# Attention of batch 0 in a fused attention and MLP kernel: split casts of x, the last exp and its sums in halves, reordered evictions and W1 copies, first MLP matmuls in two rows

## The chip, the cores and the metric

The kernel runs on one core of one Trainium2 chip. The metric is device time in microseconds (us), the median of several executions. TensorE is called PE here, VectorE DVE, ScalarE ACT, GpSimd POOL. PE multiplies matrices into PSUM banks; DVE and ACT move results out of PSUM ("evictions"); POOL does elementwise work and issues most of the loads.

A ratio is the mean time of one kernel's fast runs over the mean of the other's fast runs of the same rounds, so it is not quite the ratio of the medians that stand beside it.

## The reference, cut to what matters

```python
# attention, for each batch and head: 512 tokens x against 32 state rows, D = 64
scores = (x @ state.T) / sqrt(D);  a = softmax(scores);    xread = a @ state
scores2 = (state @ x.T) / sqrt(D); a2 = softmax(scores2);  sread = a2 @ x
h_in = concat(xread, sread)            # 544 rows per batch, 8 heads * 64 = 512 columns
# MLP
h = h_in @ w_in                        # 512 -> 2048
out = (h * sigmoid(h)) @ w_out         # 2048 -> 512
```

There are 8 batches. The kernel never forms xread: it folds state and w_in into a matrix W1 per batch, and multiplies W1 by the transposed attention weights aT. So the first MLP matmuls of a batch need both aT (two halves of four heads each, `hg` 0 and 1) and W1.

## The kernel before

Batch 0 has nothing to hide behind. Its attention is laid out at the start, as a chain over all engines:

```python
    keep_busy(7, psH, "h1")             # 7 filler matmuls of 128x512 on PE
    ...                                 # cast of the state, 4 PE transposes, 4 DVE copies to stT
    keep_busy(4, psH, "h1")
    cast_x(0, nc.vector, h0=0, nh=4)    # first half of x (4 heads), float32 to bf16, 1024 columns
    pe_transpose_x(0, 0, 2, <psO>)      # 8 PE transposes into 2 banks; copies: DVE one, ACT one
    cast_x(0, nc.vector, h0=4, nh=4)    # second half
    ...
    scores(0, 0)
    exps(0, 0)                          # ACT, 512 columns
    pe_transpose_x(0, 1, 2, <psH>)      # again one copy on DVE, one on ACT
    scores(0, 1)
    exps(0, 1)
    nc.scalar.activation(warm[:], warm[:], func=SILU, bias=0.0)   # loads the SILU table
    norm(0, 0)                          # DVE sum and reciprocal, POOL multiply of 512 columns
    norm(0, 1, ((nc.gpsimd, 0, 2), (nc.vector, 2, 2)))            # multiply: half POOL, half DVE
    w1_cols(0, [(0, 256)], (nc.scalar, nc.scalar))
    ...                                 # four weight loads and the load of x(1), issued by POOL
    keep_busy(4, psO, "o")
    pe_transpose_a(0, 0, nc.vector)     # 4 PE transposes, one DVE copy to aT
    pe_transpose_a(0, 1, nc.vector)
```

The MLP of batch 0 follows:

```python
    for ft in range(NFT):               # 16 tiles of 128 hidden columns
        upto(min(ft + LEAD0[ft], ready))       # h tile = two matmuls (hg 0, hg 1), then SILU on ACT
        if ft in W0:
            w1_cols(0, [W0[ft]], both)         # next block of W1; one copy on DVE, one on ACT
        if ft == 1:
            token_sums(0)                      # two DVE reductions of 1 us, then two small ones
        if ft == 4:
            sread(0)                           # 18 matmuls, then a DVE reciprocal and 4 products
        if ft == 5:
            transpose_state()
        if ft == 6:
            evict_state(0, nc.vector)
        if ft == 8:
            evict_state(1, nc.vector)
        ...
            for tt in range(3):
                G2(0, tt, ft)                  # second MLP matmul
```

Each engine is read here as running its own instructions in the order of the program; experiment 4 shows it for DVE, where a sum whose input was ready at 7.86 us started only at 9.05, behind two copies.

The softmax here doesn't subtract the row's maximum and nothing guards it: scores larger than these inputs give would overflow.

## Time and profile before

| | before |
|---|---|
| median of 6 runs | 224.67 us (224.41 to 225.01) |
| span of the profiled run | 222.8 us |
| PE busy | 213.7 us, 96% |

PE is busy nearly all the time, and part of the busy time at the start is filler matmuls, so the attention of batch 0 is a place where its time is not useful work. The first part of the page of the kernel before, busy time of each engine with share of the span:

```profile
PE 213.7 (96%) x1491; PEld 101.2 (45%) x1491; DVE 104.7 (47%) x183; ACT 142.5 (64%) x241; POOL 46.1 (21%) x64
```

The chain of work that ended last, in order of time, kernel before. Columns: start and length in us, then engine, what it wrote, its line in the kernel, and how many instructions are merged:

```profile
1.22 3.17 PE ps_busy L129 x7
...
4.61 1.82 PE ps_busy L129 x4
...
8.04 0.60 ACT exp_nat L242
...
9.57 0.61 ACT exp_nat L242
...
10.20 0.70 DVE rs L252
...
11.32 0.80 POOL an L255
...
12.16 0.41 PE ps_at L272 x4
...
12.60 0.43 DVE aT L123
...
13.07 0.81 PE h L362 x3
13.88 0.31 PE ps_w L336 x8
...
14.61 1.90 DVE es_f L282 x2
...
17.28 0.61 DVE W L123
...
17.94 0.39 PE h L362
```

Read it from the bottom. The MLP tile at 17.94 (the fifth, "tile 4") waited for a W1 copy on DVE. That copy stood in the DVE queue behind the token sums (`es_f`). The queue had started with the W1 block at 13.88, and that block stands on PE behind all four matmuls of the first two h tiles, which waited for the second half of aT. So tile 4 hangs on the end of batch 0's attention through PE's order and the DVE queue.

What PE waited for from 12 to 30 us, kernel before (total us, times, longest):

```profile
PE ps_at L272 <- POOL an L255: 0.8, 1, 0.8
PE ps_w L336 <- DVE stT L123: 0.4, 1, 0.4
PE h L362 <- DVE W L123: 0.4, 1, 0.4
PE h L362 <- DVE aT L123: 0.3, 1, 0.3
...
```

### The profile page before, as it was taken

What the parts mean: (1) busy time and instruction counts of PE and PEld (TensorE: products, weight loads), DVE (VectorE), ACT (ScalarE), POOL (GpSimd) and SP (SyncE); (2) the same over time, 40 slices, a digit from 0 to 9 for tenths busy, and PEclk for the clock granted to TensorE, in tenths of its full rate; (3) what the DMA queues carried; (4) which work ended last, traced back from release to release, by engine and by line L of the source; (5) the groups of instructions that cost most, each with busy time, mean ns of one, the idle gap of its engine ahead of it and who ended that gap; (6) DMA issues with size and microseconds to landing.
All of it is one profiled execution on the core that took longest, in us unless ns stands there. A gap on an engine that the chain in (4) does not pass through costs nothing.

```text
span 222.8 us, 3748 instructions
## 1 busy us (share of the span) xinstructions
PE 213.7 (96%) x1491; PEld 101.2 (45%) x1491; DVE 104.7 (47%) x183; ACT 142.5 (64%) x241; POOL 46.1 (21%) x64
## 2 busy tenths in 40 slices
PE   7879899999989999999999999999999999999993
PEld 2425235445425443544444444444454445466652
DVE  4665846452975165525644382629260846010011
ACT  2555469899555985589567947695759675834410
POOL 8480001800810035001800090008000300000000
PEclk9999999999999999999999999999999999999998
DMA  6999955493376116911495138503700330111112
GB/s 184 198 205 206 211 190 174 159 228 113 96 233 139 47 47 121 306 47 47 100 250 125 50 94 242 136 3 105 177 18 35 85 108 0 47 47 50 47 47 94
DMA packets 32209, 26.78 MB, mean 120 GB/s; under 512 B 20160, under 2 KB 26048, under 8 KB 32192
## 3 DMA queue, kind: packets, MB, share of 16 engines
q1 hardware_dynamic: 25376, 14.75, 23.8%
q0 software_dynamic: 6816, 11.80, 23.6%
q8 instruction: 11, 0.18, 0.3%
q14 instruction: 6, 0.05, 0.1%
HBM read 17.37 MB, written 8.91 MB: 118 GB/s over the span
## 4 chain that ended last, share of the span: by engine, by line
PE 85%; DVE 10%; ACT 1%; issue 1%; POOL 0%; DVEq 0%; POOLq 0%
PE o L391 45%; PE h L362 24%; PE ps_w L336 4%; PE h L372 3%; PE ps_busy L129 2%; DVE es_f L282 2%; PE ps_sc L230 2%; PE o_half L413 2%; DVE rb L312 2%; PE ps_sr L303 1%; DVE stT L123 1%; DVE W L123 1%; DVE xmT L316 1%; DVE rs L252 1%; ACT exp_nat L242 1%
## 5 line engine op out<-in xcount | busy, mean ns | idle before, releaser
L391 PE MATMUL o<-w_out_sb,g 128*128 128x512 bf16 x512 | 137.6, 379 | 0.0
L383 ACT ACTIVATE g<-h 128x512 bf16<-128x512 f32 (+1 forms) x144 | 82.1, 574 | 41.4 <-PE h L362 27.2
L362 PE MATMUL h<-aT,W 128*128 128x512 bf16 x256 | 75.5, 379 | 1.9 <-DVE W L123 1.5
L391 PEld LDWEIGHTS <-g 128*128 128x128 bf16 x528 | 49.7, 98 | 58.2 <-issue 6.4
L123 DVE COPY o_sb<-o 128x512 f32<-128x512 f32 x17 | 11.8, 692 | 62.7 <-PE o L391 62.5
L362 PEld LDWEIGHTS <-W 128*128 128x128 bf16 x256 | 24.6, 98 | 32.3 <-DVE W L123 3.7
L255 POOL TENSOR_TENSOR an<-exp_nat,rc 128x512 bf16<-128x512 bf16 (+1 forms) x16 | 16.0, 1010 | 109.8 <-DVE rc L253 109.6
L123 DVE CAST W<-ps_w 128x512 bf16<-128x512 f32 (+1 forms) x31 | 20.0, 675 | 18.7 <-PE ps_w L336 18.7
L121 ACT ACTIVATE W<-ps_w 128x512 bf16<-128x512 f32 (+1 forms) x35 | 18.7, 575 | 11.4 <-PE ps_w L336 11.3
L312 DVE RECIPROCAL rb<-ps_sr 128x256 f32<-128x256 f32 x8 | 14.0, 1749 | 16.2 <-PE ps_sr L303 16.2
L121 ACT ACTIVATE o_sb<-o 128x512 f32<-128x512 f32 x15 | 8.9, 596 | 14.3 <-PE o L391 6.1
L282 DVE TENSOR_REDUCE es_f<-exp_nat 128x128 f32<-128x512 bf16 x16 | 15.5, 1011 | 0.2
L100 POOL CAST x_nat<-x_f 128x512 bf16<-128x512 f32 x24 | 14.7, 648 | 0.0
L336 PE MATMUL ps_w<-w_in_sb,stT 64*32 64x512 bf16 (+1 forms) x264 | 11.7, 376 | 0.6 <-DVE stT L123 0.4
L252 DVE TENSOR_REDUCE rs<-exp_nat 128x16 f32<-128x512 bf16 x16 | 10.6, 660 | 1.9 <-ACT exp_nat L242 1.2
L95 POOL DMA_DIRECT2D x_f<-in_x_dram x7 | 6.5, 926 | 19.8 <-DVE x_nat L100 18.3
L316 DVE TENSOR_TENSOR xmT<-ps_sr,rb 64x64 bf16<-64x64 f32 x32 | 9.6, 299 | 0.6
L372 PE MATMUL h<-xmT,w_in_sb 128*128 128x256 bf16 x64 | 9.6, 272 | 0.0
L242 ACT ACTIVATE exp_nat<-ps_sc 128x512 bf16<-128x512 f32 x16 | 8.8, 594 | 0.9 <-PE ps_sc L230 0.8
L372 PEld LDWEIGHTS <-w_in_sb 128*128 128x128 bf16 x64 | 6.3, 98 | 3.9
L242 ACT ACT_TABLE_LOAD x6 | 7.7, 1283 | 0.1
L537 ACT ACT_TABLE_LOAD x6 | 7.7, 1283 | 0.1
(56 smaller groups left out, 102.7 us busy)
## 6 DMA issues: line engine op xcount, KB each, us to landing
out_dram<-o_sb SPq DMA_DIRECT2D x33, 256.0 KB, 2.4
x_f<-in_x_dram POOLq DMA_DIRECT2D x7, 1024.0 KB, 6.7
w_in_sb<-in_moe_w_in_dram POOLq DMA_DIRECT2D x3, 512.0 KB, 10.2
w_out_sb<-in_moe_w_out_dram POOLq DMA_DIRECT2D x3, 512.0 KB, 12.0
x_f<-in_x_dram SPq DMA_DIRECT2D x2, 512.0 KB, 4.5
w_in_sb<-in_moe_w_in_dram POOLq DMA_DIRECT2D x2, 256.0 KB, 7.3
w_out_sb<-in_moe_w_out_dram POOLq DMA_DIRECT2D x2, 256.0 KB, 7.8
st_b<-in_state_dram POOLq DMA_DIRECT2D x1, 256.0 KB, 12.1
```

The lines of the kernel that those rows point to most:

```text
L100: eng.tensor_copy(x_nat[b][:, ds(c0, nc_), ds(h0, nh), :], x_f[:, ds(h0, nh), ds(c0, nc_), :].rearrange("p h c d -> p c h d"),)
L121: nc.scalar.activation(dst, src, func=COPY, bias=0.0)
L123: eng.tensor_copy(dst, src)
L242: nc.scalar.activation(e[:], sc_ps[hg][:], func=EXP, bias=0.0, scale=SCALE)
L255: eng.tensor_tensor(a[:, ds(c, n)], e[:, ds(c, n)], rc[:, ds(c, n)].to_broadcast([128, n, 4, NS]), op=MULT,)
L282: nc.vector.tensor_reduce(f[:, hg], exp_nat[b, hg].rearrange("p c s n -> p s n c"), axis=AX, op=ADD)
L312: nc.vector.reciprocal(rb[:], ps[:, 1, :, :, :])
L336: nc.tensor.matmul(pss[f, hg][ds(32 * s, 32), 0:n], stT[ds(r, 64), b, h // 2, s % 2, :], w_in_sb[ds(r, 64), h // 2, ds(f, n)], start=True, ...
L362: nc.tensor.matmul(ps[:], W1[b][:, hg, ds(128 * ft, 128)], aT[b][:, hg, :, :], start=(hg == 0), stop=(hg == 1), skip_group_check=True,)
L372: nc.tensor.matmul(ps[:, 0:256], w_in_sb[:, kt, ds(128 * ft, 128)], xmT[:, :, kt].rearrange("p t n b -> p t (n b)"), start=(kt == 0), stop ...
L383: nc.scalar.activation(g[:, 0:n], ps[:, 0:n], func=SILU, bias=0.0)
L391: nc.tensor.matmul(outs[tt][:], gt[b * NFT + ft][:, ds(128 * tt, 128)], w_out_sb[:, ft, :], start=(ft == 0), stop=(ft == NFT - 1), skip_gr ...
```

## The change

The intent is to shorten the attention of batch 0. Both casts of batch 0's x are split in two, so that transposes can start on the first part; the exps and sums of the last half are cut in halves, so that the sum overlaps the exp. The evictions of the second half's transposes all go to DVE, W1's first copies go ahead of the SILU table load, POOL gets less of the last multiply. The fillers are moved rather than saved: 7 and 4 at the front become 4 and 5, and 2 are put in ahead of the last transposes (15 in both kernels). The first row (hg 0) of the first two h tiles is put ahead of the wait for the second half of aT.

```diff
-        eng.tensor_copy(
+        copy(
+            eng,                       # in cast_x: ACT can now do it too
@@
-    keep_busy(7, psH, "h1")
+    keep_busy(4, psH, "h1")
@@
-    keep_busy(4, psH, "h1")
+    keep_busy(5, psH, "h1")
@@
-    cast_x(0, nc.vector, h0=0, nh=4)
+    cast_x(0, nc.vector, 0, 2, 0, 4)
+    cast_x(0, nc.scalar, 2, 2, 0, 4)
     pe_transpose_x(0, 0, 2, ...)
-    cast_x(0, nc.vector, h0=4, nh=4)
+    cast_x(0, nc.vector, 0, 2, 4, 4)
+    cast_x(0, nc.vector, 2, 2, 4, 4)
@@
+    def g1_half(k, hg):                # one row (hg) of h tile k
+        b, ft = divmod(k, NFT)
+        if hg == 0:
+            h_ps[k] = psH.tile([128, 512], FP32, tag="h1", name="h1")
+        nc.tensor.matmul(h_ps[k][:], W1[b][:, hg, ...], aT[b][:, hg, :, :],
+                         start=(hg == 0), stop=(hg == 1), ...)
@@
+    pe_transpose_x(0, 1, 2, new_h, (nc.vector, nc.vector), (0,))
     scores(0, 0)
     exps(0, 0)
-    pe_transpose_x(0, 1, 2, ...)
+    pe_transpose_x(0, 1, 2, new_h, (nc.vector, nc.vector), (1,))
     scores(0, 1)
-    exps(0, 1)
+    exps(0, 1, 2)                      # in two halves
+    norm(0, 0)
+    norm(0, 1, ((nc.vector, 0, 3), (nc.gpsimd, 3, 1)), 2)    # sums in two halves
+    w1_cols(0, [(0, 256)], (nc.scalar, nc.scalar))
     nc.scalar.activation(warm[:], warm[:], func=SILU, bias=0.0)
-    norm(0, 0)
-    norm(0, 1, ((nc.gpsimd, 0, 2), (nc.vector, 2, 2)))
-    w1_cols(0, [(0, 256)], (nc.scalar, nc.scalar))
@@
     keep_busy(4, psO, "o")
     pe_transpose_a(0, 0, nc.vector)
+    keep_busy(2, psO, "o")
     pe_transpose_a(0, 1, nc.vector)
+    g1_half(0, 0)
+    g1_half(1, 0)
```

More of the change, by code (lines that the diff above doesn't have):

```diff
@@ L172, with pe_transpose_x @@
             )
-    keep_busy(4, psH, "h1")
-    def pe_transpose_x(b, hg, nb=2, new=bank, engs=(nc.vector, nc.scalar)):
+    keep_busy(5, psH, "h1")
+    def pe_transpose_x(b, hg, nb=2, new=bank, engs=(nc.vector, nc.scalar), only=None):
         if b not in xT:
@@ L181, in pe_transpose_x @@
         m = 4 // nb
-        for u in range(nb):
+        for u in range(nb) if only is None else only:
             ps = new([128, m, 2, 128], BF16, "ps_xt")
@@ L237, in scores, with exps, norm @@
                 )
-    def exps(b, hg):
+    def exps(b, hg, n=4):
         e = att.tile([128, 4, 4, NS], BF16, tag="exp", name="exp_nat")
         exp_nat[b, hg] = e
-        nc.scalar.activation(e[:], sc_ps[hg][:], func=EXP, bias=0.0, scale=SCALE)
+        for c in range(0, 4, n):
+            nc.scalar.activation(
+                e[:, ds(c, n)], sc_ps[hg][:, ds(c, n)], func=EXP, bias=0.0, scale=SCALE
+            )
     an = {}
-    def norm(b, hg, parts=((nc.gpsimd, 0, 4),)):
+    def norm(b, hg, parts=((nc.gpsimd, 0, 4),), nr=4):
         e = exp_nat[b, hg]
@@ L251, in norm @@
         an[b, hg] = a
-        nc.vector.tensor_reduce(rs[:], e[:], axis=AX, op=ADD)
+        for c in range(0, 4, nr):
+            nc.vector.tensor_reduce(rs[:, ds(c, nr)], e[:, ds(c, nr)], axis=AX, op=ADD)
         nc.vector.reciprocal(rc[:], rs[:])
@@ L355 @@
     outs = {}
+    h_ps = {}
+    def g1_half(k, hg):
+        b, ft = divmod(k, NFT)
+        if hg == 0:
+            h_ps[k] = psH.tile([128, 512], FP32, tag="h1", name="h1")
+        nc.tensor.matmul(
+            h_ps[k][:],
+            W1[b][:, hg, ds(128 * ft, 128)],
+            aT[b][:, hg, :, :],
+            start=(hg == 0),
+            stop=(hg == 1),
+            skip_group_check=True,
+        )
     def emit_G1(k):
         b, ft = divmod(k, NFT)
-        ps = psH.tile([128, 512], FP32, tag="h1", name="h1")
         if b < B:
-            for hg in range(2):
-                nc.tensor.matmul(
-                    ps[:],
-                    W1[b][:, hg, ds(128 * ft, 128)],
-                    aT[b][:, hg, :, :],
-                    start=(hg == 0),
-                    stop=(hg == 1),
-                    skip_group_check=True,
-                )
+            if k not in h_ps:
+                g1_half(k, 0)
+            g1_half(k, 1)
+            ps = h_ps.pop(k)
         else:
+            ps = psH.tile([128, 512], FP32, tag="h1", name="h1")
             for kt in range(4):
@@ L432, in upto @@
             done[0] += 1
+    new_h = lambda sh, dt, nm: psH.tile(sh, dt, tag="h1", name=nm)
+    pe_transpose_x(0, 1, 2, new_h, (nc.vector, nc.vector), (0,))
     scores(0, 0)
     exps(0, 0)
-    pe_transpose_x(0, 1, 2, lambda sh, dt, nm: psH.tile(sh, dt, tag="h1", name=nm))
+    pe_transpose_x(0, 1, 2, new_h, (nc.vector, nc.vector), (1,))
     scores(0, 1)
-    exps(0, 1)
+    exps(0, 1, 2)
+    norm(0, 0)
+    norm(0, 1, ((nc.vector, 0, 3), (nc.gpsimd, 3, 1)), 2)
+    w1_cols(0, [(0, 256)], (nc.scalar, nc.scalar))
     nc.scalar.activation(warm[:], warm[:], func=SILU, bias=0.0)
-    norm(0, 0)
-    norm(0, 1, ((nc.gpsimd, 0, 2), (nc.vector, 2, 2)))
-    w1_cols(0, [(0, 256)], (nc.scalar, nc.scalar))
     load_w_in(1024)
```

## The prediction

> **What bounds the kernel now.** The page gives TensorE (PE) 213.7 of 222.8 us busy; only idle or filler PE time can be won. The change touches batch 0 before 15 us. There the chain that ended last (in order of time) runs: fillers `ps_busy` x7 to 4.39, state transposes to 4.60, fillers x4 to 6.42, x transposes, an ACT copy of xT 7.06-7.66, scores, exp 8.04-8.64, ACT copy of xT 8.63-9.19, scores, exp 9.57-10.17, DVE sum 10.20-10.90, reciprocal to 11.19, POOL multiply 11.32-12.12, transposes, DVE copy of aT 12.60-13.03, first MLP matmuls 13.07.
>
> **What the change removes and moves (timeline durations).**
> 1. Fillers 7 to 4, then 4 to 5. State transposes can start at about 3.1 instead of 4.32, since the state cast ends at 2.98. The x transposes start near 5.4 instead of 6.22. The first half of x lands at about 4.8; its cast, halved over DVE and ACT, takes about 0.42 and 0.60 instead of 0.69.
> 2. But PE now transposes the second half's first two chunks before scores(0,0). That half of x lands only at about 7.16 (the DVE cast started at 7.18). So the 0.8 us is lost in waiting: scores(0,0) moves from 7.32 to about 7.9, its exp from 8.04 to about 8.35.
> 3. The second half gains: cast in two parts of 0.42, both xT copies on DVE (0.42 against ACT's 0.60). The last exp starts at about 9.37 instead of 9.57.
> 4. exp and sum in halves overlap: sums end near 10.65 instead of 10.90, the reciprocal near 10.9 instead of 11.17. The first half's later exp makes POOL's full multiply run 10.1-11.1 (before 9.83-10.88). POOL's last part shrinks from 256 columns (0.79) to 128, estimated 0.66 from the 512-column 1.05: it ends near 11.75 instead of 12.11. DVE's three chunks end near 11.5.
> 5. W1 copies move ahead of the 1.28 us SILU table load, off the path. First-row matmuls of two tiles move ahead of the wait for the second aT: two of 0.216 us starts leave the path.
>
> **On the critical path.** Transposes of `an` gain about 0.35; the first SILU the same (13.49 to about 13.12). The second h tile and the W1 block behind it gain about 0.6, which starts the DVE queue (W1 cast, token sums 1.97 us, W1 cast) about 0.6 earlier; PE waits 0.37 for it at 17.94, so from there the whole gain should be about 0.6. No weight load becomes the limit: the third w_in block lands at 21.95, wanted at about 22.2.
>
> **Predicted: 223.95 us, 8 in 10 between 223.2 and 224.8. Faster by over 2%: 0.01; within 2%: 0.98; slower: 0.01.**
>
> **What would show it.** PE first x transpose near 5.4; an idle gap of over 1 us ending near 7.65 on the second cast; exp(0,0) starting near 8.35, the last exp near 9.4, first SILU near 13.1, first G2 near 13.8, MLP tile 4 near 17.35 instead of 17.94.
>
> **What would make it wrong.** (a) x landing later or earlier. (b) The clock: before, filler starts are 427 ns apart, and from about 6.6 us transposes go from 107 to 56 ns. The Trainium skill, "TensorE: Matmul & The Clock Gate", Part 1, says that the clock opens after one busy, free-running window of about 3.4 us. The new PE gap near 6.2-7.65 could leave it cold to 10 us in some runs, costing 0.3-1 us. (c) POOL multiply longer than estimated. (d) The third w_in block landing late, capping the gain at 0.9.

## The result, and the profile after

| | before | after |
|---|---|---|
| median of 6 runs | 224.67 us (224.41 to 225.01) | 224.00 us (223.74 to 224.34) |
| span of the profiled run | 222.8 us | 222.1 us |
| PE busy | 213.7 us | 213.2 us |

The ratio is 0.997, with a 95% interval of 0.9957 to 0.9983: a small gain, within 2%. Run again as a control on the chip of later experiments, the kernel after gave 224.14 us against 224.71 us (ratio 0.9976, 0.996 to 0.9993).

The first part of the page, kernel after:

```profile
PE 213.2 (96%) x1491; PEld 101.4 (46%) x1491; DVE 105.6 (48%) x186; ACT 142.6 (64%) x242; POOL 45.5 (20%) x64
```

The chain of work that ended last, kernel after, same columns:

```profile
1.68 5.21 DMA x_f<-in_x_dram
...
6.91 0.44 DVE x_nat L124
...
7.40 0.54 PE ps_xt L187 x4
7.94 0.23 PE ps_sc L233 x8
8.17 0.24 PE ps_xt L187 x4
...
8.43 0.43 DVE xT L124
...
9.24 0.67 ACT exp_nat L246 x2
...
9.97 1.06 POOL an L262
...
11.07 0.40 PE ps_at L279 x4
11.47 0.43 PE ps_busy L130 x2
11.90 0.24 PE ps_at L279 x4
...
12.64 0.59 PE h L370 x2
13.23 0.31 PE ps_w L343 x8
...
13.95 1.90 DVE es_f L289 x2
...
16.63 0.61 DVE W L124
...
17.29 0.60 PE h L370 x2
```

The chain now begins with a DMA: the landing of x's second half at 6.89. The fillers at the front are off it. Between the landing and the first SILU every engine has a piece. One link of this view misleads: it puts the last exp before POOL's multiply at 9.97, but that multiply is of the first half. In the timelines it starts 0.15 to 0.16 us after the first half's reciprocal ends (9.81 here), and in the kernel before it starts at 9.83, before the last exp ends at 10.17. The last transposes start inside the piece at 11.90 (their first start is 11.74 in the timeline); tile 4 starts at 17.29 instead of 17.94.

What PE waited for from 12 to 30 us, kernel after:

```profile
PE ps_w L343 <- DVE stT L124: 0.4, 1, 0.4
PE o L408 <- ACT g L400: 0.2, 1, 0.2
...
PE h L370 <- DVE W L124: 0.2, 1, 0.2
```

The waits of 0.8 for POOL's last multiply and of 0.3 for the second half of aT are gone from this list, and the wait for DVE's W1 copy has shrunk from 0.4 to 0.2. A new wait of 0.2 for the first SILU has appeared. The wait of 0.4 for `stT`, later in the MLP, has merely moved with the rest.

From tile 4 on the offset is carried to the end: start of h tile 8's SILU -0.65, of tile 64's SILU -0.66, end of the span -0.66. Nothing is won or lost behind the head in this pair.

### The profile page after: what moved, and what is told of

Its sections match the earlier page's. It is cut to its first block, busy times and chain, and to the rows that moved or that the text cites. A ratio compares the mean times of both kernels' runs of the same rounds, so it can differ in the third digit from the quotient of the medians.

```text
span 222.1 us, 3753 instructions
## 1 busy us (share of the span) xinstructions
PE 213.2 (96%) x1491; PEld 101.4 (46%) x1491; DVE 105.6 (48%) x186; ACT 142.6 (64%) x242; POOL 45.5 (20%) x64
## 4 chain that ended last, share of the span: by engine, by line
PE 84%; DVE 9%; DMA 2%; ACT 1%; issue 1%; POOL 0%; SPq 0%; DVEq 0%; ACTq 0%
PE o L408 45%; PE h L370 24%; PE ps_w L343 4%; PE h L389 3%; DMA x_f<-in_x_dram 2%; PE ps_sc L233 2%; DVE es_f L289 2%; PE o_half L430 2%; DVE rb L319 2%; PE ps_sr L310 1%; DVE stT L124 1%; DVE W L124 1%; DVE xmT L323 1%; PE ps_xt L187 1%; PE ps_sr L300 1%; PE o_a L408 1%
## 5 line engine op out<-in xcount | busy, mean ns | idle before, releaser
L262 POOL TENSOR_TENSOR an<-exp_nat,rc 128x512 bf16<-128x512 bf16 (+2 forms) x16 | 15.9, 1004 | 109.8 <-DVE rc L260 106.1
L259 DVE TENSOR_REDUCE rs<-exp_nat 128x16 f32<-128x512 bf16 (+1 forms) x17 | 10.6, 629 | 1.5 <-ACT exp_nat L246 0.6
L246 ACT ACTIVATE exp_nat<-ps_sc 128x512 bf16<-128x512 f32 (+1 forms) x17 | 8.9, 569 | 1.4 <-PE ps_sc L233 1.3
```

The costliest lines, as they stand in the source:

```text
L246: nc.scalar.activation(e[:, ds(c, n)], sc_ps[hg][:, ds(c, n)], func=EXP, bias=0.0, scale=SCALE)
L262: eng.tensor_tensor(a[:, ds(c, n)], e[:, ds(c, n)], rc[:, ds(c, n)].to_broadcast([128, n, 4, NS]), op=MULT,)
```

## The experiments

The tool for most verdicts is a small table. It cuts the head at three instants of each profile: the landing of x's second half (the last completion of that DMA in the trace), the first of the last four `ps_at` transposes on PE, and tile 4 on PE. The differences take out the landing, which scatters from run to run. "Clock opens" is where the trace's record of the granted TensorE clock goes from half to full.

| kernel | clock opens | x lands | landing to last transposes | last transposes to tile 4 | median of timed runs |
|---|---|---|---|---|---|
| before | 6.61 | 7.16 | 5.00 | 5.78 | 224.67 |
| after | 7.74 | 6.89 | 4.85 | 5.55 | 224.00 |
| after, control | 7.49 | 7.09 | 4.92 | 5.55 | 224.14 |
| before, fillers changed | 5.82, shut 9.24 to 12.65 | 7.12 | 5.36 | 5.83 | 225.58 |
| before, two rows | 4.95 | 7.29 | 5.00 | 5.56 | 224.86 |
| after, no rows | 6.71 | 6.96 | 4.70 | 5.77 | 224.21 |
| after, scores first | 4.99 | 7.43 | 4.50 | 5.54 | 224.00 |
| after, no halves | 5.10 | 7.10 | 4.71 | 5.55 | 224.71 |
| after, whole casts | 14.22 | 7.25 | 6.71 | 5.68 | 224.46 |
| after, more fillers | 4.65 | 7.09 | 4.72 | 5.54 | 224.12 |

The last column is from three chips. In the runs of the same rounds the kernel before had 225.16 (fillers changed, two rows, no rows), 224.71 (control, scores first, no halves, whole casts) and 225.10 (more fillers).

My theory going in: the gain is the earlier last transposes (about 0.35) plus the rows, which start the DVE queue earlier (about 0.25). Rivals: the removed fillers are the gain; or the first SILU alone decides.

### 1. Only the fillers

```diff
 # the kernel before
-    keep_busy(7, psH, "h1")
+    keep_busy(4, psH, "h1")
-    keep_busy(4, psH, "h1")
+    keep_busy(5, psH, "h1")
```

> The kernel before with only the filler counts of the change (7 to 4, then 4 to 5). My theory: no gain in the total (within 0.15 us of before). The x transposes start near 5.8 instead of 6.22 and the first exp near 7.6 instead of 8.04, but the last exp stays near 9.5, because it hangs on the landing of x's second half near 6.9-7.2 and its undivided cast. Rival: the fillers stood on the chain of waits with 3.17 and 1.82 us, so removing some of them is the main source of the gain: 0.4 us or more.

Measured: 225.58 us against 225.16, ratio 1.0022 (0.9994 to 1.005), and a wide scatter, 224.59 to 226.56. The rival falls: the front fillers alone give no gain. But "no change" was not right either. The x transposes started at 6.63, not near 5.8, because the first half of x landed at 5.52 in this run (4.77 in the kernel before) and its cast took 1.04 us instead of 0.69. And the profile shows a cost. Busy time by stretch of this kernel (columns: stretch and length, busy us and count of PE, PEld, DVE, ACT, POOL, then the granted clock, DMA share and GB/s; the clock column does not count the time ahead of the first opening):

```profile
2.41:5.82 3.41, 3.14 (x11) 0.76 (x9) 1.66 (x6) 0.00 (x0) 3.41 (x5) 1.00 0.95 292
5.82:9.23 3.41, 1.99 (x29) 1.41 (x28) 2.42 (x5) 1.56 (x3) 0.88 (x2) 1.00 1.34 207
9.23:12.64 3.41, 3.27 (x26) 1.48 (x24) 2.14 (x6) 2.80 (x6) 2.05 (x3) 0.50 1.29 205
```

The clock opened at 5.82. In the stretch that followed PE's instructions covered 1.99 of 3.41 us, and for the next 3.41 us the clock was at half. The Trainium skill, "TensorE: Matmul & The Clock Gate", Part 1, describes this: a free-running window of about 3.4 us in which PE's activity is judged. The trace agrees on the length: the open stretches of the clock record are multiples of 3.413 us (215.04 is 63 of them). By this estimate one lost window costs a mean clock of 0.5 * 3.41 / 222 = 0.008, so a run listed at 0.992 lost one and a run near 0.984 two. Four of the six runs here are at 0.983 to 0.992; those four took 225.51 to 226.56, the other two 224.59 and 224.96. In 44 timed runs of the kernel before the lowest is 0.997.

Some of the loss in this profile lies later: a wait of 0.29 us at 53.34 for a DMA (see experiment 5).

### 2 and 3. The two rows, added to before and taken from after

```diff
 # the kernel before, with g1_half and emit_G1 of the kernel after
     pe_transpose_a(0, 1, nc.vector)
+    g1_half(0, 0)
+    g1_half(1, 0)
```

> The kernel before with only the two-row first MLP matmuls. My theory: the first SILU and the first G2 stay where they were (13.49 and 14.14), but the second h tile and the W1 block behind it come 0.2 us earlier, the DVE queue starts 0.2 us earlier, and PE's wait at 17.94 for the W1 cast shrinks from 0.37 to about 0.15: total gain about 0.2 us. Rival: the gain follows the first SILU alone; then this run gains nothing.

```diff
 # the kernel after
-    g1_half(0, 0)
-    g1_half(1, 0)
```

> The kernel after without the two-row first MLP matmuls. My theory: first SILU stays near 13.05, W1 block at about 13.38 instead of 13.16, MLP tile 4 at about 17.5 instead of 17.29; about 0.2 us slower than the kernel after (gain against before 0.45 instead of 0.65). Rival: as fast as the kernel after.

Measured: the rows on before gave 224.86 against 225.16 (ratio 0.999, 0.9973 to 1.0008); after without rows 224.21 against the same 225.16 (0.9973, 0.9945 to 1.0001). The totals point the expected way but cannot resolve 0.2 us. The profiles can. In the table the step from last transposes to tile 4 has two values only, wherever the clock is open: 5.77 to 5.78 without rows, 5.54 to 5.56 with them. The rows are worth 0.22 us, in both directions. The PE wait for DVE's W1 copy, timeline of PE, after without rows:

```profile
17.43 0.61 PE L370 MATMUL h<-aT,W 128*128 128x512 bf16 x2 [0.37 <-DVE W L124]
```

and of the kernel after:

```profile
17.29 0.60 PE L370 MATMUL h<-aT,W 128*128 128x512 bf16 x2 [0.16 <-DVE W L124]
```

The bracket is PE's idle time and who ended it. The rows made it 0.16 instead of 0.37, although the first SILU is no earlier with them: it follows the last transposes by 1.31 in the kernel after and by 1.32 without rows. So the first SILU does not decide; the start of the DVE queue does.

### The control

The kernel after itself, on the chip of experiments 4 to 6:

> The kernel after, unchanged, as a control on the chip of these runs, and a second profile of it. In the first profiles x's second half landed at 6.89 in the kernel after and in the others with divided casts at 6.66 to 6.96, against 7.12 to 7.29 in the three with whole casts. If the landing is chance, it should scatter over 6.6 to 7.3 here and in the three beside it; the last multiply's transposes should follow the landing by 4.85 (before: 5.00). Total 0.5 to 0.8 us below before.

Measured: 224.14 against 224.71, ratio 0.9976 (0.996 to 0.9993). x landed at 7.09, and at 7.10 to 7.43 in the three beside it, so the landing scatters, though a little later than I allowed for. The last transposes followed by 4.92, hardly better than before's 5.00: the 4.85 was no constant, and part of the first profile's gain was a lucky landing. The timelines show where the two profiles of the kernel after lose against the 4.70 to 4.72 of the variants whose clock opened early. In the first, the second half's transposes ran partly at half clock, and the first xT copy behind them started 0.58 us after them, not 0.43. In the control, the first half's transposes took 1.03 us at half clock (0.62 from the same start in the kernel without halves), so their xT copy on DVE ended late and the cast of the second half, behind it in the queue, started 0.26 us after the landing, not 0.05. Two of the six runs, 224.60 and 224.95, have a mean clock of 0.992; the other four are at 223.90 to 224.21.

### 4. scores(0,0) back ahead of the second half's transposes

```diff
 # the kernel after
-    pe_transpose_x(0, 1, 2, new_h, (nc.vector, nc.vector), (0,))
     scores(0, 0)
     exps(0, 0)
+    pe_transpose_x(0, 1, 2, new_h, (nc.vector, nc.vector), (0,))
     pe_transpose_x(0, 1, 2, new_h, (nc.vector, nc.vector), (1,))
```

> The kernel after with scores(0,0) and its exp put back ahead of the second half's transposes on PE. My theory: the first exp starts at about 7.6 instead of 8.21, but the DVE queue still does the sum of that half only after its two xT copies (8.84), so nothing comes earlier behind it; the second half's transposes even start 0.1 to 0.15 later: total 0 to 0.15 us slower than the kernel after. Rival, as my prediction's step 2 has it (time lost in waiting for the second half of x): 0.4 us or more faster than the kernel after.

The first profile: 278.97 us at a granted clock of 0.757; nothing is read from it. The five fast runs were 223.54 to 224.08, ratio 0.9942 (0.9924 to 0.996), but without the kernel after beside them. So it was run again, with the control:

> The kernel with scores(0,0) first once more, since its profile fell in a slow state with a granted clock of 0.757, while its five fast runs gave 223.9. Theory: the first exp near 7.6 to 7.8 instead of 8.21, the first sum still near 8.8 behind the two xT copies, total within 0.15 us of the kernel after beside it. Rival: 0.4 us or more faster than it.

Measured: 224.00 against the control's 224.14 and before's 224.71 (ratio 0.997, 0.9945 to 0.9994). The first exp starts at 7.26, almost a microsecond earlier than in the kernel after (8.21), on ACT:

```profile
7.26 0.60 ACT L246 ACTIVATE exp_nat<-ps_sc 128x512 bf16<-128x512 f32 x1 [0.38 <-PE ps_sc L233]
```

and yet its sum on DVE comes at 9.05, because the queue holds it behind the two xT copies:

```profile
8.37 0.76 DVE L124 COPY xT<-ps_xt 128x512 bf16<-128x512 bf16 x2 [0.16 <-PE ps_xt L187]
9.05 0.68 DVE L259 TENSOR_REDUCE rs<-exp_nat 128x16 f32<-128x512 bf16 x1
```

So most of what step 2 of the prediction called lost is not lost: the early exp had nowhere to go. The rival's 0.4 did not appear, though the intervals of the totals do not exclude it. My own expectation (0 to 0.15 slower) did not hold either: the last transposes follow the landing by 4.50 here, against 4.70 to 4.72 in the three other variants of the kernel after whose clock was open early. The trace has the reason: PE no longer runs eight score matmuls between the two groups of transposes, so the two xT copies take 0.76 us on DVE instead of 0.88, and the sum behind them no longer waits for the first exp, which in the kernel after ends at 8.81, just before its sum at 8.84. So the order that the change chose costs about 0.2 us in the head. One profile shows it, and the totals (0.14 apart) do not resolve it.

### 5. The last exp and its sum undivided

```diff
-    exps(0, 1, 2)
+    exps(0, 1)
-    norm(0, 1, ((nc.vector, 0, 3), (nc.gpsimd, 3, 1)), 2)
+    norm(0, 1, ((nc.vector, 0, 3), (nc.gpsimd, 3, 1)))
```

> The kernel after with the last exp and its sum undivided. Theory: the second reciprocal ends about 0.13 later (10.83 instead of 10.70), but POOL is still busy with the first half's multiply until 11.0, so the last transposes stay near 11.74 and the total does not move (within 0.1). Rival: the halves are a main part of the 0.35 gained on that chain; then 0.15 us or more slower than the kernel after.

In the head the theory holds. The second reciprocal ends at 10.93, but POOL's two multiplies run without a pause:

```profile
10.05 1.73 POOL L262 TENSOR_TENSOR an<-exp_nat,rc 128x512 bf16<-128x512 bf16 x2 [3.44 <-ACT exp_nat L246]
```

The last transposes follow the landing by 4.71, just as in the variants that have the halves. The halves hide behind POOL's first multiply and buy nothing in this profile. DVE's multiply shows how: here, without the halves,

```profile
10.96 0.56 DVE L262 TENSOR_TENSOR an<-exp_nat,rc 128x384 bf16<-128x384 bf16 x1
```

and in the kernel after, which has them,

```profile
10.73 0.70 DVE L262 TENSOR_TENSOR an<-exp_nat,rc 128x384 bf16<-128x384 bf16 x1
```

the one with the earlier start takes longer, and both end 0.42 us after POOL's first multiply ends (11.09 and 11.01).

The totals say otherwise: 224.71, ratio 0.9999 (0.9972 to 1.0026), against the control's 0.9976; one of the six runs is 226.41. For the profiled run of 224.57 us the trace shows where its time went. At the SILU of tile 24 it was 0.19 ahead of the control, at that of tile 32 it was 0.20 behind. In between PE waited for the DMA transpose of batch 2's x (timeline of PE, this kernel):

```profile
52.37 0.64 PE L233 MATMUL ps_sc<-stT,xT 128*128 128x64 bf16 x16 [0.27 <-DMA xT<-x_nat]
```

A shorter head does not explain it: the kernel after reached tile 24 earlier (47.52 against 47.61) without this wait, and experiment 1 met it with a longer head (48.55). It follows the transfer's own time: 9.28 to 9.33 us from issue to landing in the three profiles that have the wait (this one, experiment 1 and the first of experiment 8), 8.71 to 9.09 in the ten others. So this loss does not belong to the halves. What made the run of 226.41 slow was not profiled, so the totals leave it open whether the halves are worth something.

### 6. Casts undivided

```diff
-    cast_x(0, nc.vector, 0, 2, 0, 4)
-    cast_x(0, nc.scalar, 2, 2, 0, 4)
+    cast_x(0, nc.vector, h0=0, nh=4)
-    cast_x(0, nc.vector, 0, 2, 4, 4)
-    cast_x(0, nc.vector, 2, 2, 4, 4)
+    cast_x(0, nc.vector, h0=4, nh=4)
```

> The kernel after with both casts of x undivided on DVE. Theory: the second half's transposes start 0.27 later after its landing (0.69 of cast instead of 0.42) and the last transposes follow the landing by about 5.1 instead of 4.85; 0.2 to 0.3 us slower than the kernel after. Rival: the divided casts also let x land earlier; then x's second half lands at 7.1 to 7.3 here, and the loss is 0.4 to 0.6.

Measured: 224.46 against the control's 224.14; ratio to before 0.9997 (0.9967 to 1.0027). The size fits the theory. One piece of it stands in the profile: the undivided cast took 0.68 us where the first part of a divided one takes 0.42. The rest cannot be confirmed: in the profiled run, 226.52 us, the clock opened only at 14.22. The filler matmuls tell it by their pace: two in 1.06 us on PE in this kernel,

```profile
13.11 1.06 PE L130 MATMUL ps_busy<-busy 128*128 128x512 bf16 x2
```

two in 0.59 us in the kernel after:

```profile
11.30 0.59 PE L130 MATMUL ps_busy<-busy 128*128 128x512 bf16 x2
```

The rival (divided casts let x land earlier) finds no support: with divided casts x landed at 7.09, 7.10 and 7.43 in the runs beside this one, with whole casts at 7.25. The earlier pattern looks like chance.

The listed mean clock does not see such a late opening: it counts only what is lost after the first opening, and this run is listed at 1.0. Three unprofiled runs of the changed head are listed at 1.0 too and lie 1.5 to 1.7 us above the medians of their kernels: 225.57 (scores first), 225.73 (no rows) and 226.41 (no halves). A late opening would fit them, but it is not shown. No run of the kernel before lies more than 0.6 above its median.

### 7. More fillers, to test the lost clock windows

```diff
 # the kernel after
+    keep_busy(2, psH, "h1")
     pe_transpose_x(0, 1, 2, new_h, (nc.vector, nc.vector), (0,))
```

> The kernel after with two fillers put into PE's wait for x's second half. So far runs with the changed head lost a clock window now and then (mean granted clock 0.992 in 2 of 6 runs of the control; opening only at 14.2 us in the profile of the undivided casts), the kernel before never. Theory: these are windows in which PE was too idle, so with the fillers all runs show 0.996 or more, none is over 224.7, and the median stays within 0.15 us of the kernel after (two cold fillers end near 7.4, where x's second half is only just cast). Rival: the lost windows are chance of the chip; then they come as often here.

Measured: 224.12 against 225.10 (0.9968, 0.9949 to 0.9988). No run is under 0.997, but one took 225.25, so the expectation of none over 224.7 failed. The changed head, in all its variants without these two fillers, showed a mean clock of 0.992, a window lost after the first opening, in 4 of 47 fast runs (two of the control, one without rows, one with whole casts); this kernel and the later ones with the fillers in none of 18. That is too few to settle it, and a simple threshold does not fit either. A stretch in which PE's instructions covered 2.84 of 3.41 us (kernel after, 0.91 to 4.32) did not open the clock; one with 2.85 (control, 4.08 to 7.49) did, and so did the next one of the kernel after, with 2.76 (4.33 to 7.74). What the rule is stays open. That thinning PE's head work can cost a window is shown by experiment 1 alone.

### 8. The next wait on the DVE queue

Experiments 2 and 3 say that PE's limit behind the head is the DVE queue. So the work in it was moved:

```diff
 # the kernel after
     for ft in range(NFT):
+        if ft == 3:
+            sread(0)
         upto(min(ft + LEAD0[ft], ready))
         ...
-        if ft == 4:
-            sread(0)
-        if ft == 5:
+        if ft == 4:
             transpose_state()
-        if ft == 6:
+        if ft == 5:
             evict_state(0, nc.vector)
-        if ft == 8:
+        if ft == 6:
             evict_state(1, nc.vector)
```

> The kernel after with the work behind the DVE queue moved earlier: sread(0) ahead of MLP tile 4, the state transposes and evictions one to two steps earlier. Theory (the DVE queue is what PE waits for after the head): PE's waits at 17.29 (0.16), 22.78 (0.6) and 27.19 (0.45) shrink, unless the third w_in block (landing 21.9) becomes the limit: 0.6 to 1.2 us faster than the kernel after, so near 223. Rival: PE's idle time is only moved to a later wait; within 0.2 us of the kernel after.

Measured: 223.41 against 225.10, ratio 0.9932 (0.9912 to 0.9952), so 0.7 us better than 224.12 with more fillers in the same rounds; the kernel after itself was not in them. PE's waits from 12 to 40 us in this kernel:

```profile
PE h L370 <- DVE W L124: 0.3, 1, 0.3
PE o L408 <- ACT g L400: 0.2, 1, 0.2
PE o L408 <- issue: 0.2, 1, 0.2
```

The 0.4 for `stT` is gone. The edit moves sread's 18 matmuls on PE as well as the work on DVE, and the trace shows how it acts: DVE, which had been idle for 2.46 us before sread's reciprocal at 19.69 in the kernel after, idles 0.63 us and starts it at 18.00. With the fillers added as well:

> Both of the above together: if they are independent, the median of the version with the earlier sread, without slow windows (all runs within 0.5 us of each other).

Measured: 223.36 (222.69 to 223.66), ratio 0.9922 (0.9905 to 0.9939).

One wait stands in every profile so far: 0.86 to 1.10 us between 62 and 66 us, where batch 2's first tile needs W1 copies that stand on DVE behind a reciprocal, products and token sums.

```diff
 # the version with both
-                        w1_chunks(n, (0, 1), both)
+                        w1_chunks(n, (0, 1), both if b > 1 else (nc.scalar, nc.scalar))
```

> The version with the earlier sread and the fillers, with one more wait on the DVE queue taken away: in batch 1 all four W1 copies of batch 2's first two blocks go to ACT, which is idle there, instead of two standing at the end of the DVE queue behind reciprocal, products and token sums. In every profile so far PE waits about 1.0 us near 62 to 63 for them (1.08 in the version it is built on). Theory: that wait falls under 0.2 and the total by 0.9 to 1.1 us, ratio to before near 0.988. Rival: the wait moves to the next thing in the same stage (aT's transfer, or the following W1 blocks); gain under 0.4.

PE at that place in the version with both (timeline):

```profile
62.57 0.60 PE L370 MATMUL h<-aT,W 128*128 128x512 bf16 x2 [1.08 <-DVE W L124]
```

and with the copies on ACT:

```profile
61.31 0.59 PE L370 MATMUL h<-aT,W 128*128 128x512 bf16 x2
```

Measured: 222.08 us (221.65 to 223.00) against 224.88, ratio 0.9881 (0.9861 to 0.9902). The wait is gone and no new one appeared in that stage. Earlier, at 22.19, PE now waits 0.19 us for the third w_in block, which landed at 22.15. The version with both had been 1.7 us under before of its rounds; this one is 2.8 us under its own, and beats both kernels, where the change alone had won 0.6 to 0.7. All outputs were correct in all the experiments.

## Why the prediction was right or wrong

It was right in size: 223.95 predicted, 224.00 measured, and gains of 0.67 and, in the control, 0.57 beside the predicted "about 0.6".

- **Whole gain about 0.6, carried to the end unchanged.** Right. The offset at tile 8 and at the end differ by 0.01 in the first pair.
- **The rows are worth a quarter of a microsecond and act through the DVE queue.** Right; this was the surest part. 0.22 measured in both directions, and PE's wait at tile 4 went from 0.37 to 0.16.
- **0.35 on the chain to the last transposes.** The first profile shows 0.42 (12.16 to 11.74), but for the wrong reason: 0.27 of it is an earlier landing of x in that run. From the landing on, the gain is 0.15, and 0.08 in the control. Where the clock was open by 7.0 us, it is 0.28 to 0.30 (4.70 to 4.72 against 5.00), and the three profiles of experiment 8 agree (4.71 to 4.73). So this term was too large where the clock opens late, and near enough where it opens early. Which edit gives how much of it is only partly known: the casts were tried in a profile with a late clock, and the evictions on DVE, the order of the W1 copies and POOL's smaller part were not tried alone. That the timed gain, 0.57 to 0.67, is nearer the sum for an open clock (0.30 + 0.22) is what the runs allow to say; the clock of the timed runs ahead of its opening was not recorded.
- **Step 1, x transposes near 5.4.** They started at 5.69: the state cast took 0.69 instead of 0.41 (see below), and its end moved to 3.31. It did not matter in that run, because the first half had slack until the second half landed. In the control it had none: there the first half landed at 5.56, not at 4.8, and its late xT copy held up the cast of the second half by 0.26.
- **Step 2, "the 0.8 us is lost in waiting".** The instants were near (a gap of 0.65 ending at 7.40, where over 1 us ending at 7.65 was predicted; exp at 8.21 for 8.35), the word lost was mostly wrong. Experiment 4 moved the first exp almost a microsecond earlier, and the last transposes gained only 0.2 after the landing.
- **Step 4, halves overlap.** The overlap exists, but experiment 5 shows in the head that it is behind POOL's multiply of the first half. The POOL part took 0.71 (estimated 0.66), and DVE's three chunks 0.70 where the predicted instants (10.9 to 11.5) leave 0.6. The sizes came out near, but not for the reason given: the prediction lets the two engines multiply side by side, and the traces show them taking turns. In the ten profiles with this split, DVE's 384 columns end 0.41 to 0.45 us after POOL's 512 columns end, whenever they started, and POOL's 128 columns end 0.26 us after DVE's. So 0.71 is mostly waiting, and the chain to the last transposes runs through all three multiplies.
- **Risk (b), the clock.** It is real: 2 of 6 control runs lost a window after the clock had opened (224.60 and 224.95, the other four 223.90 to 224.21). The prediction had a cost of 0.3 to 1 us "in some runs"; that holds here. The late opening that it described shows in the profiled run with whole casts, at 2.1 us above the median of its kernel.
- **Risk (d), the third weight block.** It did not bind in the kernel after: it landed at 21.90. It did in the last version of experiment 8, by 0.19.

A word on DVE's surprising durations, which the profiles show and no run here was made to isolate. The first 512-column cast of x took 0.46 when it began 0.60 us into POOL's issue of a weight load (4.50 to 5.31), and 0.72 when it began 0.32 us into one. DVE in the kernel after:

```profile
5.10 0.46 DVE L124 CAST x_nat<-x_f 128x512 bf16<-128x512 f32 x1 [0.61 <-DMA x_f<-in_x_dram]
```

DVE and POOL in the control:

```profile
5.58 0.72 DVE L124 CAST x_nat<-x_f 128x512 bf16<-128x512 f32 x1 [1.10 <-DMA x_f<-in_x_dram]
5.26 0.79 POOL L118 DMA_DIRECT2D w_out_sb<-in_moe_w_out_dram  x1
```

All profiles fit one rule. DVE casts that began 0.25 to 0.60 us into an issue of a weight load ended late: the first 512 columns of x 1.04 to 1.06 us after the issue began, wherever they started. Those that began 0.08 to 0.24 us into one took no longer than alone, and then the issue was often the longer one: in the kernel before, where the cast of 1024 columns started 0.12 after POOL's issue of the same load, the issue took 1.11 instead of 0.79. The Trainium skill, "SBUF — State Buffer", section "Who interferes with whom", says that DVE in a two-port mode, which casts can enter, and GpSimd exclude each other, the first to come blocking the other fully, and it counts GpSimd's making of DMA descriptors among the work that is blocked. These durations agree with it. The multiplies of `an` in step 4 take turns in the same way.

## What to carry to other kernels

Cut a head at the instants that do not depend on luck (a landing, a transpose, the first tile) and compare the pieces: totals that scatter by 0.3 us cannot resolve changes of 0.2, and a single pair of profiles credits the change with an early DMA. Before shortening a step, look where its consumer stands in the queue of the next engine: the exp that came almost a microsecond earlier gained 0.2 us in the head and the halved sums nothing there, while feeding the DVE queue earlier gained about 0.7 us and moving two copies off it about 1 us, with a few lines. Look also whether two engines that should work side by side take turns, as DVE and POOL do here. Filler matmuls off the chain may still hold up the clock, so removing them needs several runs and a look at the clock of each.

## What the Trainium skill lacked or had wrong

- "TensorE: Matmul & The Clock Gate", Part 1, under HAM oscillation, gives the rule as no PE idle gaps over about 3.4 us. Here that was not enough: in experiment 1 the clock shut at 9.24 although PE's longest wait in the window was 0.73 us; PE's instructions covered 1.99 of its 3.41 us.
- The same part does not say how busy a window must be to open the clock. Here windows covered to 2.69 (79%) and 2.41 (71%) of 3.41 us left it shut in the run with whole casts, 2.85 opened it in the control, and in the kernel after 2.84 left it shut and 2.76 opened it. No threshold on covered time fits all runs: after a window covered to 1.99 of 3.41 us, the clock shut in experiment 1; at 1.95 (5.10 to 8.51, no halves) and 1.79 (4.26 to 7.67, the version with both) it stayed open.
- "SBUF — State Buffer", "Who interferes with whom", does not say which part of a DMA issue on POOL blocks DVE. Here casts that began up to 0.24 us into a weight load's issue were not slowed, and those that began 0.25 to 0.60 us into one were held.
